# Attention values of two heads by turns, with the softmax sums divided out behind them

## The chip, the cores and the metric

The kernel runs on one core of a Trainium2 chip. The metric is the device time of one execution in microseconds, lower is better. The engines work side by side, each through its own list of instructions in a fixed order: TensorE (PE), VectorE (DVE), ScalarE (ACT), GpSimd (POOL), and SyncE (SP), which issues most DMAs.

## The reference

Sliding-window attention with a few sink keys, then two feed-forward layers, the first with a rational function, the second with a sigmoid. All in fp32.

```python
# q, k, v: 2 batches, 8 heads, 768 tokens, 64 wide; 4 sinks, window 128
scores = scale * np.matmul(q, k.transpose(0, 1, 3, 2))
keep = is_sink | in_window
scores = np.where(keep, scores, -1000000000.0)
scores = scores - np.max(scores, axis=-1, keepdims=True)
a = np.exp(scores)
a = a / (np.sum(a, axis=-1, keepdims=True) + 1e-09)
attn_out = np.matmul(a, v)
x = attn_out.transpose(0, 2, 1, 3).reshape(1536, 512)
# layer 1: w_in 512 x 2048, w_out 2048 x 512
h = x @ w_in
g = (a0 + a1*h + a2*h2 + a3*h3) / (1 + |b0|*|h| + |b1|*h2 + 1e-6)
x = g @ w_out
# layer 2, the same shapes
h = x @ w_in2
out = (h / (1 + np.exp(-1.702 * h))) @ w_out2
```

## The kernel before

The 1536 tokens are taken in three blocks of 512 (`TB`), each four query blocks of 128. Attention of a block runs over four pairs of heads. For a pair, `scores` multiplies the queries with the keys that a query block sees: its own 128, the 128 before and 16 sink columns, 272 in all (128 for the first query block of a batch). The two heads lie on the two halves of the 128 partitions and their scores are taken by turns. DVE adds the mask and takes the maximum (`m`, `nm`), ACT the exponential into `a` with its sum in `sm`. `normalise` adds a small number to the sums, takes the reciprocal `rs`, and multiplies every row of `a` by it, on DVE or POOL; the sink columns are also copied into a dense tile `as`. `transposes` turns blocks of 128 x 128 of `a` around on PE, three to a PSUM tile (`GROUP`), the sink tile as one more of them; ACT or DVE copy them into `th` and `sT`. `values` multiplies them with `vr`: output is 64 x 128 to 64 x 512, one head in the lower, one in the upper half of one PSUM tile, first all products of the one head, then all of the other, then the sinks of both. The result is split into a high part `xh` (ACT) and a rest `xl` (DVE) for the feed-forward layers (called MoE in the code), which multiply in three passes (high by high, high by rest, rest by high).

The layers run over units of one block and half or all of the 16 slices of the inner dimension (`UNITS`). Their weights arrive by DMA as 64-bit numbers (`wraw`), one tile of 512 KB at a time into two buffers, and are decoded on ACT (`dy`), DVE (`dy`, `dt`, and the rest into `wi` or `wo`) and one of three engines (the high part). The elementwise work of layer 1 (`y`, `z`, `s`, `r`, `gh`, `gl`) lies on ACT and DVE, with one DMA of POOL that adds.

The order of all instructions is found when the kernel is built: `play` goes through a list of operations with costs and priorities (the longest way to the end plus a number from `BIAS` for each group) and lets each engine start what is ready. That order is then written out for all five engines, SP's DMAs too. Some operations may go to one of several engines (`WH`, `SN`, `TH`, `S2`, `ST`); the plan decides. Where PE would have nothing in the first stage, the plan puts filler matmuls (`acc<-zero`, 256 columns) that only keep it busy. Extra buffers for the layers open once attention has ended. In tile names the number of the buffer is left out in the profile; in the order the number behind a name tells tiles apart.

Of the kernel before, what the change touches and what calls it, by code (L numbers as in the profile page):

```python
# [5 lines left out]
F32 = mybir.dt.float32  # L6
# [4 lines left out]
ALU = mybir.AluOpType  # L11
PSUM = bass.MemoryType.PSUM
DRAM = bass.MemoryType.DRAM
# [26 lines left out]
GROUP = 3  # L40
# [3 lines left out]
A_BUFS, M_BUFS, T_BUFS, VR_BUFS, KQ_BUFS = 4, 3, 6, 4, 2  # L44
# [5 lines left out]
TH, SN, PE_OUT = "act/dve", "pool/dve", "act/dve"  # L50

BIAS = {
# [4 lines left out]
}  # L57
HEAD = (5.08, 0.16, 15.06, 0.34)
THETA = -0.68
# [17 lines left out]
class View:  # L77
# [66 lines left out]
class Program:  # L144
# [56 lines left out]
    def op(self, eng, meth, alloc=(), alts=(), given=False, calls=(), cost=0.0, **kw):  # L201
# [18 lines left out]
        if calls:  # L220
            runs = [runner(eng, meth, c) for c in calls]
            o.alts = {eng: (cost, lambda: [f() for f in runs][-1])}
            o.cost, o.lat = cost, PE_LAT
            o.columns = sum(c["rhs"].n * 4 * (c["lhsT"].box[0][1] - c["lhsT"].box[0][0]) / P for c in calls)
        elif meth == "dma_start":
            v = views[0][1]
            o.nbytes = (v.box[0][1] - v.box[0][0]) * v.n * 4
            o.cost, o.lat = 0.45 if v.box[0][1] - v.box[0][0] == P else 0.62, DMA_LAT
            if eng == "gpsimd":
                o.nbytes *= 2  # L230
                o.cost, o.lat = ADD_FIX, ADD_LAT + 0.6 * (kw["out"].dtype == F32R)
            o.alts = {eng: (o.cost, runner(eng, meth, kw))}
        else:
            self.columns = 0
            o.alts = {e: (self.price(e, m_, k_), runner(e, m_, k_)) for e, m_, k_ in [(eng, meth, kw)] + list(alts)}
            o.cost = min(c for c, _ in o.alts.values())
            o.columns = self.columns
            if eng == "tensor":
                o.lat = PE_LAT
# [262 lines left out]
def emit(tc, qT, kX, vL, w_in, w_out, ca, cb, nw, out):  # L502
# [344 lines left out]
    def build_banded():  # L847
        with (
# [4 lines left out]
            tc.tile_pool(name="ps", bufs=1, space=PSUM) as ps,  # L853
        ):
# [16 lines left out]
            def attention(T, xs, alone):  # L871
# [28 lines left out]

                near = {k: [q for q in (k, (k[0], k[1] + 1)) if q in qcol] for k in kbs}
                n_g = -(-(sum(len(l) for l in near.values()) + bool(sq)) // GROUP)
                used = [0] * n_g
                place = {}
                for k in sorted(kbs, key=lambda k: -len(near[k])) + (["s"] if sq else []):
                    w = len(near[k]) if k != "s" else 1
# [39 lines left out]
                def scores(h):  # L946

                    kr, qr = st.pop(("kq", h // 2))
                    t = []
                    for e in (h, h + 1):  # L950
                        a = R.tile(ap, [P, 4, 2 * P + SC], F32, tag="a", name="a", bufs=A_BUFS)
                        nm = R.tile(ap, [P, 4], F32, tag="nm", name="nm", bufs=5)
                        sm = R.tile(ap, [P, 4], F32, tag="sm", name="sm", bufs=5)
                        st["a", e] = a, sm
                        t.append((slice((e % 2) * D, (e % 2 + 1) * D), a, nm, sm))
                    for i, (b, qb) in enumerate(qs):
                        off, w = (P + SC, P) if qb == 0 else (0, 2 * P + SC)
                        k0 = kcol[b, max(0, qb - 1)] * KW
                        ps_ = [pst("s") for _ in t]
                        R.op("tensor", "matmul", alloc=[x for y in t for x in y[1:]], cost=w / 420 + 0.11, calls=[  # L960
                            dict(out=p[:, :w], lhsT=qr[r, i * P:(i + 1) * P], rhs=kr[r, k0:k0 + w], start=True, stop=True)
                            for p, (r, _, _, _) in zip(ps_, t)])
                        for p, (_, a, nm, sm) in zip(ps_, t):
# [4 lines left out]
                            R.op("scalar", "activation", out=a[:, i, off:off + w], in_=mt[:, :w], func=AF.Exp, scale=-1.0,  # L968
                                 bias=nm[:, i:i + 1], accum_out=sm[:, i:i + 1])

                def normalise(h):
                    a, sm = st["a", h]
                    rs = R.tile(ap, [P, 4], F32, tag="rs", name="rs", bufs=2)
                    R.op("vector", "tensor_scalar", out=rs[:, :nq], in0=sm[:, :nq], scalar1=EPS_SM, scalar2=None, op0=ALU.add)
                    R.op("vector", "reciprocal", out=rs[:, :nq], in_=rs[:, :nq])
                    for i, (b, qb) in enumerate(qs):
                        off = P + SC if qb == 0 else 0
                        affine(SN, a[:, i, off:], a[:, i, off:], rs[:, i:i + 1], 0.0)
                    if sq:
                        i0, i1 = qcol[sq[0]], qcol[sq[-1]] + 1  # L980
                        s2 = R.tile(ap, [P, 4, 2 * SC], F32, tag="as", name="s2", bufs=2)
                        hi(S2, s2[:, :i1 - i0], a[:, i0:i1, P:P + 2 * SC])
                        st["s2", h] = s2[:, :i1 - i0]

                def transposes(h):
                    a, sm = st.pop(("a", h))
                    tr = []
                    for g in range(n_g):
                        t = R.tile(ap, [P, GROUP * P], F32, tag="th", name="th", bufs=T_BUFS)
                        p = pst("t")  # L990
                        w, ns = used[g] * P, 0
                        for k, (g2, at) in place.items():
                            if g2 != g:
                                continue
                            if k == "s":
                                ns = len(sq) * 2 * SC
                                R.op("tensor", "transpose", alloc=(t,), out=p[:ns, at * P:w], in_=st.pop(("s2", h)), identity=ident)
                                continue
# [3 lines left out]
                        if ns:  # L1002
                            w -= P
                            sT = R.tile(ap, [SC, 4 * P], F32, tag="sT", name="sT", bufs=2)
                            for j in range(len(sq)):
                                hi(ST, sT[:, j * P:(j + 1) * P], p[2 * SC * j:2 * SC * j + SC, w:w + P])
                            st["sT", h] = sT
# [4 lines left out]
                def values(h):  # L1012

                    x = pst("v")
                    calls, vrs = [], []
                    for e in (h, h + 1):
                        r0 = (e % 2) * D
                        p, tr, vr = x[r0:r0 + D], st.pop(("T", e)), st.pop(("v", e))
                        vrs.append(vr)
                        ops = []  # L1020
                        for k in first + later:
                            (g, at), n = place[k], len(near[k])
                            q0 = qcol[near[k][0]]
                            ops.append((p[:, q0 * P:(q0 + n) * P], vr[:, vcol[k], :], tr[g][:, at * P:(at + n) * P]))
                        for j, (o, l, r) in enumerate(ops):
                            calls.append(dict(out=o, lhsT=l, rhs=r, start=(j == 0), stop=(not sq and j == len(ops) - 1)))
                    if sq:
                        for e in (h, h + 1):
                            q0, n = qcol[sq[0]] * P, len(sq) * P
                            calls.append(dict(out=x[(e % 2) * D:(e % 2 + 1) * D, q0:q0 + n], lhsT=vrs[e % 2][:SC, vcol[sq[0][0], "s"], :], rhs=st.pop(("sT", e))[:, :n], start=False, stop=True))  # L1030
                    cost = sum(c["rhs"].n / 1100 + COL_EACH for c in calls)
# [166 lines left out]
```

## Time and profile before

| | us |
|---|---|
| median of 3 runs | 692.75 |
| lowest, highest | 690.96, 694.33 |
| profiled execution, its own time | 695.05 |
| its span, first to last instruction | 692.9 |
| mean granted clock of TensorE | 0.986 |

The page gives each engine's busy time. The table of windows gives the same by stretch, with the number of instructions; the timeline gives starts and durations in order of time (the distance from one start to the next is what an instruction costs its engine, since durations overlap); the groups give count, busy time and mean duration of instructions of one kind.

### The profile page before, as it was taken

To read this page: it belongs to the slowest core of one execution; us is meant where nothing else is said; L and a number is where in the kernel's file an instruction comes from. 1 tells how busy PE (TensorE), PEld (TensorE's weight loads), DVE (VectorE), ACT (ScalarE), POOL (GpSimd) and SP (SyncE) were. 2 spreads that over 40 slices of the span, in tenths; PEclk is the share of its full clock that TensorE was granted. 3 is DMA by queue.
4 is the path that set the end of the run, shared out by engine and by line. 5 is a ranking of instruction groups with operands and counts; after the bars stand their busy time and mean duration, and the time that the engine had idled before them with its cause. 6 is when DMAs were issued, how large, how long until landed. Compare 5 with 4: busy or idle time off the path is not lost.

```text
span 692.9 us, 9131 instructions
## 1 busy us (share of the span) xinstructions
PE 670.3 (97%) x3141; PEld 518.0 (75%) x3141; DVE 518.8 (75%) x1101; ACT 380.0 (55%) x786; POOL 102.2 (15%) x144
## 2 busy tenths in 40 slices
PE   7999999999999999999899999999999999999995
PEld 6776666677667787867687888788888888878874
DVE  5999999887686999997999999985488633131341
ACT  3686888687666775665767755543354422132220
POOL 1533342121121322111213100100000000000000
PEclk7999999999999999999999999999999999999998
DMA  5565766522211454344425324443033200010011
GB/s 164 172 188 148 197 171 165 128 68 53 54 32 30 92 125 104 77 107 122 86 66 140 58 60 118 124 125 92 17 105 122 62 1 0 1 48 13 16 46 64
DMA packets 29862, 61.69 MB, mean 89 GB/s; under 512 B 5744, under 2 KB 11888, under 8 KB 29808
## 3 DMA queue, kind: packets, MB, share of 16 engines
q1 hardware_dynamic: 22608, 48.44, 23.0%
q0 software_dynamic: 6912, 12.59, 10.8%
q8 instruction: 26, 0.43, 0.3%
q14 instruction: 28, 0.23, 0.1%
q10 hardware_dynamic: 288, 0.00, 0.0%
HBM read 45.29 MB, written 3.15 MB: 70 GB/s over the span
## 4 chain that ended last, share of the span: by engine, by line
PE 75%; DVE 7%; issue 6%; ACT 5%; DMA 5%; POOL 1%; SPq 0%; DVEq 0%; POOLq 0%; ACTq 0%
PE att L215 26%; PE acc L215 24%; PE h L215 19%; DMA z<-y 3%; PE att L216 3%; PE acc L863 2%; DVE s L216 2%; DVE dt L216 1%; ACT th L216 1%; DVE gl L216 1%; DMA q<-q_t 1%; ACT r L216 1%; DVE z L216 1%; ACT a L216 1%; ACT sT L216 1%
## 5 line engine op out<-in xcount | busy, mean ns | idle before, releaser
L215 PE MATMUL h<-xh,wi 128*128 128x512 f32 x448 | 151.5, 396 | 2.2 <-DVE s L216 1.7
L215 PE MATMUL att<-xh,wi 128*128 128x512 f32 x320 | 106.7, 391 | 0.0
L215 PE MATMUL acc<-gh,wo 128*128 128x512 f32 x288 | 100.6, 404 | 3.3 <-ACT wo L216 2.2
L215 PEld LDWEIGHTS h<-xh,wi 128*128 128x128 f32 x448 | 83.8, 188 | 26.1 <-issue 3.1
L216 DVE SCALAR_TENSOR_TENSOR dt<-wraw,dt 128x512 int32<-128x512 int32 x128 | 87.9, 688 | 1.4
L215 PE MATMUL h<-xl,wi 128*128 128x512 f32 x224 | 88.0, 393 | 0.0
L215 PE MATMUL acc<-wo,gh 128*128 128x512 f32 x256 | 83.2, 394 | 0.0
L216 DVE TENSOR_TENSOR gl<-y,gh 128x512 fp32r<-128x512 f32 x48 | 32.8, 689 | 66.7 <-PE acc L215 54.9
L215 PEld LDWEIGHTS att<-xh,wi 128*128 128x128 f32 x320 | 60.1, 188 | 14.2 <-DVE s L216 0.2
L216 POOL DMA_DIRECT2D z<-y x48 | 42.3, 887 | 192.5 <-ACT z L216 175.1
L215 PEld LDWEIGHTS acc<-gh,wo 128*128 128x128 f32 x288 | 53.6, 189 | 19.3 <-ACT wo L216 3.0
L215 PE MATMUL att<-xl,wi 128*128 128x512 f32 x160 | 62.5, 391 | 0.0
L216 ACT ACTIVATE dy<-wraw 128x512 f32<-128x512 f32 x64 | 42.9, 671 | 29.7 <-DMA wraw<-w_out 19.6
L216 ACT ACTIVATE a<-m,nm 128x272 f32<-128x272 f32 (+1 forms) x96 | 47.3, 496 | 19.1 <-DVE nm L216 18.9
L215 PE MATMUL acc<-gl,wo 128*128 128x512 f32 x144 | 55.5, 403 | 1.5 <-DVE gl L216 1.4
L215 PEld LDWEIGHTS acc<-wo,gh 128*128 128x128 f32 x256 | 48.0, 188 | 11.2 <-ACT wo L216 0.2
L216 ACT ACTIVATE r<-z,ln_b 128x512 f32<-128x512 f32 x48 | 34.6, 722 | 33.5 <-DMA z<-y 33.4
L216 ACT ACTIVATE gh<-y 128x512 fp32r<-128x512 f32 x48 | 30.2, 629 | 33.7 <-PE acc L215 25.2
L215 PEld LDWEIGHTS h<-xl,wi 128*128 128x128 f32 x224 | 42.1, 188 | 8.5 <-issue 0.4
L215 PE MATMUL att<-wo,gh 128*128 128x512 f32 x128 | 47.6, 396 | 0.4 <-POOL wo L216 0.3
L215 PE MATMUL acc<-wo,gl 128*128 128x512 f32 x128 | 45.6, 393 | 0.0
L216 DVE SCALAR_TENSOR_TENSOR gh<-s,a_t,r 128x512 fp32r<-128x512 f32 x48 | 36.0, 751 | 11.5 <-ACT r L216 10.5
(126 smaller groups left out, 1227.7 us busy)
## 6 DMA issues: line engine op xcount, KB each, us to landing
wraw<-w_in SPq DMA_DIRECT2D x32, 512.0 KB, 3.7
wraw<-w_out SPq DMA_DIRECT2D x32, 512.0 KB, 3.7
z<-y POOLq DMA_DIRECT2D x48, 256.0 KB, 3.3
vr<-v_l SPq DMA_DIRECT2D x16, 160.0 KB, 3.4
q<-q_t SPq DMA_DIRECT2D x8, 256.0 KB, 3.6
out<-xf SPq DMA_DIRECT2D x8, 256.0 KB, 2.4
k<-k_x SPq DMA_DIRECT2D x4, 360.0 KB, 3.1
k<-k_x SPq DMA_DIRECT2D x4, 288.0 KB, 5.0
```

The lines of the kernel that those rows point to most:

```text
L215: return getattr(e, meth)(a.pop("out"), **a)
L216: return getattr(e, meth)(**a)
L863: nc.tensor.matmul(R.real[k][:, 0:256], lhsT=zero[:, :P], rhs=zero, start=True, stop=True)
```

## The change

`values` takes the two heads by turns: product for product, first head, second head. The rows of `a` are no longer scaled; `normalise` is gone. Instead `sums` takes the reciprocals of the eight sums per partition of a pair (two heads, four query blocks), transposes them on PE to eight rows of 128, copies them to `rt`, writes them to DRAM (`rd`) and reads them back with two DMAs, each of which spreads one head's 512 numbers over 64 partitions (`rb`). DVE multiplies the values in PSUM by `rb`, and `xh` and `xl` are made from the product. `sinks` transposes the sink columns of each query block by themselves, straight from `a`, 32 columns at a time, into a PSUM tile of their own, so that one copy takes a pair (two copies where a block has four such query blocks). Four blocks go to one PSUM tile instead of three. There are fewer buffers for `m` and `th`; outside block 0 the transposes stand behind the pair's last scores. `BIAS`, `HEAD` and `THETA` have other numbers, so that the whole order differs.

```diff
-GROUP = 3
+GROUP = 4
-A_BUFS, M_BUFS, T_BUFS, VR_BUFS, KQ_BUFS = 4, 3, 6, 4, 2
+A_BUFS, M_BUFS, T_BUFS, VR_BUFS, KQ_BUFS = 4, 2, 4, 4, 2
-    "at0": 57.37, "at1": 40.94, "at2": -26.39, "at3": -86.3, "m0": -5.97, "m1": 87.68, "m2": 11.75,
+    "at0": 30.94, "at1": 72.58, "at2": 21.27, "at3": -64.03, "m0": -7.08, "m1": 59.83, "m2": 7.83,
...
+    def spread(self, n):
+        return View(self.t, self.box, self.dims, self.steps + [
+            lambda v: v.rearrange("(o a) b -> o (a b)", o=1).to_broadcast([n, v.shape[0] * v.shape[1]])], self.dtype)
...
-                def normalise(h):
-                    a, sm = st["a", h]
-                    rs = R.tile(ap, [P, 4], F32, tag="rs", name="rs", bufs=2)
-                    R.op("vector", "tensor_scalar", out=rs[:, :nq], in0=sm[:, :nq], scalar1=EPS_SM, scalar2=None, op0=ALU.add)
-                    R.op("vector", "reciprocal", out=rs[:, :nq], in_=rs[:, :nq])
-                    for i, (b, qb) in enumerate(qs):
-                        off = P + SC if qb == 0 else 0
-                        affine(SN, a[:, i, off:], a[:, i, off:], rs[:, i:i + 1], 0.0)
-                    if sq:
-                        i0, i1 = qcol[sq[0]], qcol[sq[-1]] + 1
-                        s2 = R.tile(ap, [P, 4, 2 * SC], F32, tag="as", name="s2", bufs=2)
-                        hi(S2, s2[:, :i1 - i0], a[:, i0:i1, P:P + 2 * SC])
-                        st["s2", h] = s2[:, :i1 - i0]
+                def sums(h):
+                    sm = st.pop(("sm", h))
+                    rs = R.tile(ap, [P, 8], F32, tag="rs", name="rs", bufs=2)
+                    R.op("vector", "tensor_scalar", out=rs, in0=sm, scalar1=EPS_SM, scalar2=None, op0=ALU.add)
+                    R.op("vector", "reciprocal", out=rs, in_=rs)
+                    p = pst("t")
+                    R.op("tensor", "transpose", out=p[:8, :P], in_=rs, identity=ident)
+                    rt = R.tile(ap, [8, P], F32, tag="rt", name="rt", bufs=2)
+                    hi(ST, rt, p[:8, :P])
+                    rd = R.tile(dp, [8, P], F32, tag="rd", name="rd", bufs=4)
+                    R.op("sync", "dma_start", out=rd, in_=rt)
+                    rb = R.tile(ap, [P, 4 * P], F32, tag="rb", name="rb", bufs=2)
+                    for e in (0, 1):
+                        R.op("sync", "dma_start", out=rb[e * D:(e + 1) * D], in_=rd[4 * e:4 * e + 4].spread(D))
+                    st["rb", h] = rb
+
+                def sinks(h):
+                    n, G = len(sq), 2 * SC
+                    t = R.tile(ap, [SC, 8 * P], F32, tag="sT", name="sT", bufs=1)
+                    for es in [(0, 1)] if n <= 2 else [(0,), (1,)]:
+                        p = pst("t")
+                        o = R.op("tensor", "transpose", alloc=(t,), cost=len(es) * n * 0.109 + 0.1, calls=[
+                            dict(out=p[:G, (i * n + j) * P:(i * n + j + 1) * P], in_=st["a", h + e][:, qcol[q], P:P + G], identity=ident)
+                            for i, e in enumerate(es) for j, q in enumerate(sq)])
+                        if not alone:
+                            R.in_order([st["last", h], o])
+                        hi(ST, t[:, es[0] * n * P:(es[-1] + 1) * n * P], p[:SC, :len(es) * n * P])
+                    st["sT", h] = t
...
                 def values(h):
...
+                    for k in first + later:
+                        (g, at), n = place[k], len(near[k])
+                        q0 = qcol[near[k][0]]
+                        ops += [(e, q0, n, vrs[e][:, vcol[k], :], tiles[e][g][:, at * P:(at + n) * P]) for e in (0, 1)]
...
                     n, c = nq * P, h // 2
-                    hi(XH, xs[0][c][:, :n], x[:, :n])
-                    lo("dve", xs[1][c][:, :n], x[:, :n], xs[0][c][:, :n])
+                    rb = st.pop(("rb", h))
+                    tt("dve", ALU.mult, rb, x[:, :n], rb)
+                    hi(XH, xs[0][c][:, :n], rb)
+                    lo("dve", xs[1][c][:, :n], rb, xs[0][c][:, :n])
...
-                        items.append(lambda h=2 * r - 2: (normalise(h), transposes(h), normalise(h + 1), transposes(h + 1), values(h)))
+                        items.append(lambda h=2 * r - 2: (sums(h), sinks(h) if sq else 0, transposes(h), transposes(h + 1), values(h)))
```

PE, the products of the first pair of block 0, before (`vr_62` and `vr_63` are the two heads):

```order
L215 MATMUL h_432<-th_379,vr_62 64x256
L215 MATMUL h_432<-th_388,vr_62 64x256
L215 MATMUL h_432<-th_396,vr_62 64x256
L215 MATMUL h_432<-th_379,vr_62 64x128
L215 MATMUL h_432<-th_406,vr_63 64x256
L215 MATMUL h_432<-th_418,vr_63 64x256
L215 MATMUL h_432<-th_416,vr_63 64x256
L215 MATMUL h_432<-th_406,vr_63 64x128
L215 MATMUL h_432<-sT_386,vr_62 64x256
L215 MATMUL h_432<-sT_411,vr_63 64x256
```

And now, the same products:

```order
L220 MATMUL h_348<-th_283,vr_62 64x256
L220 MATMUL h_348<-th_332,vr_63 64x256
L220 MATMUL h_348<-th_283,vr_62 64x256
L220 MATMUL h_348<-th_332,vr_63 64x256
L220 MATMUL h_348<-th_304,vr_62 64x256
L220 MATMUL h_348<-th_343,vr_63 64x256
L220 MATMUL h_348<-th_304,vr_62 64x128
L220 MATMUL h_348<-th_343,vr_63 64x128
L220 MATMUL h_348<-sT_309,vr_62 64x256
L220 MATMUL h_348<-sT_309,vr_63 64x256
```

The number and shape of the products are the same; their order goes from head after head to turn by turn. (One such row is two instructions in the trace.)

DVE in block 0 before, where the sums of one pair come in and rows of `a` are scaled between two weight decodes (`dt`):

```order
L216 TENSOR_SCALAR rs_289<-sm_283 128x4
L216 TENSOR_SCALAR dt_375<-dy_218 128x512
L216 RECIPROCAL rs_289<-rs_289 128x4
L216 TENSOR_SCALAR rs_285<-sm_294 128x4
L216 COPY sT_386<-att_357 16x128
L216 RECIPROCAL rs_285<-rs_285 128x4
L216 SCALAR_TENSOR_TENSOR dt_375<-wraw_64,dt_375 128x512
L216 TENSOR_SCALAR a_293<-a_293,rs_285 128x272
L216 SCALAR_TENSOR_TENSOR dt_375<-wraw_64,dt_375 128x512
L216 TENSOR_SCALAR a_282<-a_282,rs_289 128x272
```

And now, around the first multiplication by the spread reciprocals, which waits for its two DMAs:

```order
L221 SCALAR_TENSOR_TENSOR dt_233<-wraw_65,dt_233 128x512
L221 ISA m_207,nm_204<-acc_191,mk_125 128x272
L221 ISA nm_204 128x1
L221 TENSOR_TENSOR rb_390<-h_348,rb_390 128x512
L221 ISA m_203,nm_381<-acc_193,mk_125 128x272
L221 ISA nm_381 128x1
L221 SCALAR_TENSOR_TENSOR dt_233<-wraw_65,dt_233 128x512
```

The scalings are gone; the multiplication stands between score reductions (`m`) of later pairs and decode, so those stand behind it. Between the reciprocal of this pair and this row lie 9.5 us of other DVE work by the durations of the trace, 8.3 to 10.4 us for eleven of the twelve pairs and 5.0 us for the last.

SP in block 0 before, the loads of weights and of the next pair:

```order
L216 DMA k_181<-k_x 128x576
L216 DMA q_184<-q_t 128x512
L216 DMA wraw_64<-w_out 128x1024
L216 DMA vr_62<-v_l 128x320
L216 DMA vr_63<-v_l 128x320
L216 DMA wraw_65<-w_in 128x1024
```

And now, with the store and the two spreading loads of the first pair:

```order
L221 DMA wraw_65<-w_in 128x1024
L221 DMA rd_340<-rt_326 8x128
L221 DMA k_183<-k_x 128x576
L221 DMA q_186<-q_t 128x512
L221 DMA vr_62<-v_l 128x320
L221 DMA vr_63<-v_l 128x320
L221 DMA rb_390<-rd_340 64x512 x2
L221 DMA wraw_64<-w_out 128x1024
```

The store waits for ACT's copy, the loads for the store's landing, and the next weight load stands behind them. Of the 354 MoE matmuls that stood ahead of the last pair's values on PE, 159 still do; ahead of the eighth pair's, 75 instead of 73. Fillers go from 153 to 88.

## Rows read from the trace of the kernel before

**Rows 1.** The page: busy time of each engine, share of the span, instructions.

```profile
PE 670.3 (97%) x3141; PEld 518.0 (75%) x3141; DVE 518.8 (75%) x1101; ACT 380.0 (55%) x786; POOL 102.2 (15%) x144
```

**Rows 2.** Windows: from:to, length, busy us (instructions) by engine, clock, DMA, GB/s.

```profile
20.00:65.60 45.60, 45.19 (x304) 32.21 (x304) 44.56 (x143) 33.33 (x106) 20.73 (x30) 1.00 0.55 166
65.60:121.70 56.10, 54.44 (x321) 36.96 (x320) 54.14 (x164) 45.82 (x131) 18.97 (x27) 1.00 0.66 176
121.70:224.30 102.60, 101.04 (x504) 71.77 (x503) 79.18 (x195) 73.58 (x169) 17.05 (x25) 1.00 0.28 61
224.30:400.00 175.70, 168.77 (x717) 134.22 (x717) 167.83 (x275) 120.22 (x190) 38.37 (x45) 0.99 0.44 97
684.70:692.90 8.20, 0.00 (x0) 0.00 (x0) 1.81 (x4) 0.00 (x0) 0.00 (x0) 0.69 0.38 134
```

**Rows 3.** Timeline, DVE: the eighth pair's last operation (start, duration, instruction).

```profile
121.70 0.68 DVE L216 TENSOR_TENSOR xl<-att,xh 128x512 fp32r<-128x512 f32 x1
```

**Rows 4.** Timeline, PE: value products of one pair in blocks 0, 1 and 2.

```profile
41.70 2.65 PE L215 MATMUL h<-th,vr 128*64 128x256 f32 x16
44.28 0.65 PE L215 MATMUL h<-sT,vr 16*64 16x256 f32 x4
44.86 0.73 PE L215 MATMUL acc<-k,q 64*128 64x272 f32 x4
...
78.00 2.87 PE L215 MATMUL att<-th,vr 128*64 128x256 f32 x20
80.81 0.65 PE L215 MATMUL att<-sT,vr 16*64 16x256 f32 x4
81.38 0.73 PE L215 MATMUL att<-k,q 64*128 64x272 f32 x4
...
219.54 3.08 PE L215 MATMUL att<-th,vr 128*64 128x256 f32 x20
222.55 1.07 PE L215 MATMUL att<-sT,vr 16*64 16x512 f32 x4
223.56 0.50 PE L215 MATMUL h<-xh,wi 128*128 128x512 f32 x1
```

**Rows 5.** Timeline, PE: a sink transpose among the others, block 0.

```profile
49.34 0.27 PE L216 MATMUL att<-ident,a 128*128 128x128 f32 x1
49.45 0.27 PE L216 MATMUL att<-ident,as 128*64 128x128 f32 x1
49.56 0.49 PE L216 MATMUL att<-ident,a 128*128 128x128 f32 x3
```

**Rows 6.** Timeline, DVE: starts of operations one behind the other.

```profile
47.22 0.43 DVE L216 CUSTOM_DVE_ANT_0 m<-acc,mk 128x272 f32<-128x272 f32 x1
47.58 0.08 DVE L216 DVE_READ_ACCUMULATOR2_ANT nm<- 128x1 f32 x1
47.58 0.68 DVE L216 TENSOR_TENSOR xl<-h,xh 128x512 fp32r<-128x512 f32 x1
48.18 0.68 DVE L216 SCALAR_TENSOR_TENSOR dt<-wraw,dt 128x512 int32<-128x512 int32 x1
```

**Rows 7.** Groups of DVE up to 121.7 us: count, busy us, mean ns, idle before.

```profile
L216 DVE SCALAR_TENSOR_TENSOR dt<-wraw,dt 128x512 int32<-128x512 int32 x38 | 26.3, 695 | 0.2
...
L216 DVE TENSOR_SCALAR dy<-dy 128x512 f32<-128x512 f32 x19 | 8.5, 446 | 0.9 <-ACT dy L216 0.6
...
L216 DVE TENSOR_SCALAR a<-a,rs 128x272 f32<-128x272 f32 x17 | 7.8, 488 | 0.0
...
L216 DVE TENSOR_SCALAR a<-a,rs 128x128 f32<-128x128 f32 x9 | 3.0, 349 | 0.0
...
L216 DVE TENSOR_SCALAR rs<-sm 128x4 f32<-128x4 f32 x16 | 2.5, 180 | 0.0
```

**Rows 8.** The page, DMA issues: count, KB each, median us to landing.

```profile
out<-xf SPq DMA_DIRECT2D x8, 256.0 KB, 2.4
...
k<-k_x SPq DMA_DIRECT2D x4, 288.0 KB, 5.0
...
vr<-v_l SPq DMA_DIRECT2D x16, 32.0 KB, 2.1
...
b_t<-c_b ACTq DMA_DIRECT2D x1, 1.0 KB, 6.2
```

More of the change, by code (lines that the diff above doesn't have):

```diff
@@ L223, in op @@
             o.cost, o.lat = cost, PE_LAT
-            o.columns = sum(c["rhs"].n * 4 * (c["lhsT"].box[0][1] - c["lhsT"].box[0][0]) / P for c in calls)
+            o.columns = sum(c["rhs"].n * 4 * (c["lhsT"].box[0][1] - c["lhsT"].box[0][0]) / P if "rhs" in c else 2 * P for c in calls)
         elif meth == "dma_start":
@@ L853, in build_banded @@
             tc.tile_pool(name="ps", bufs=1, space=PSUM) as ps,
+            tc.tile_pool(name="dr", bufs=1, space=DRAM) as dp,
         ):
@@ L901, in attention @@
                 near = {k: [q for q in (k, (k[0], k[1] + 1)) if q in qcol] for k in kbs}
-                n_g = -(-(sum(len(l) for l in near.values()) + bool(sq)) // GROUP)
+                n_g = -(-sum(len(l) for l in near.values()) // GROUP)
                 used = [0] * n_g
                 place = {}
-                for k in sorted(kbs, key=lambda k: -len(near[k])) + (["s"] if sq else []):
-                    w = len(near[k]) if k != "s" else 1
+                for k in sorted(kbs, key=lambda k: -len(near[k])):
+                    w = len(near[k])
                     g = min((g for g in range(n_g) if used[g] + w <= GROUP), key=lambda g: used[g])
@@ L959, in scores @@
                         ps_ = [pst("s") for _ in t]
-                        R.op("tensor", "matmul", alloc=[x for y in t for x in y[1:]], cost=w / 420 + 0.11, calls=[
+                        o = R.op("tensor", "matmul", alloc=[sm] + [x for y in t for x in y[1:3]], cost=w / 420 + 0.11, calls=[
                             dict(out=p[:, :w], lhsT=qr[r, i * P:(i + 1) * P], rhs=kr[r, k0:k0 + w], start=True, stop=True)
                             for p, (r, _, _, _) in zip(ps_, t)])
-                        for p, (_, a, nm, sm) in zip(ps_, t):
+                        for p, (_, a, nm, s0) in zip(ps_, t):
                             mt = R.tile(ap, [P, 2 * P + SC], F32, tag="m", name="mt", bufs=M_BUFS)
@@ new lines, in scores @@
+                    st["last", h] = st["last", h + 1] = o
+                def sums(h):
+                    sm = st.pop(("sm", h))
+                    assert nq == 4
+                    rs = R.tile(ap, [P, 8], F32, tag="rs", name="rs", bufs=2)
[11 more added lines that the diff above has]
+                    st["rb", h] = rb
@@ L990, in transposes @@
                         p = pst("t")
-                        w, ns = used[g] * P, 0
+                        w = used[g] * P
+                        n0 = len(R.ops)
                         for k, (g2, at) in place.items():
                             if g2 != g:
[L994 to L997, printed above, removed]
                                 continue
@@ L1001, in transposes @@
                                 R.op("tensor", "transpose", alloc=(t,), out=p[:, (at + j) * P:(at + j + 1) * P], in_=a[:, qcol[q], o:o + P], identity=ident)
[L1002 to L1007, printed above, removed]
+                        if not alone:
+                            R.in_order([st["last", h], R.ops[n0]])
                         hi(TH, t[:, :w], p[:, :w])
@@ L1014, in values @@
                     x = pst("v")
[L1015 to L1026, printed above, removed]
@@ L1027, in values @@
-                    if sq:
[L1028 to L1031, printed above, removed]
+                    tiles = [st.pop(("T", e)) for e in (h, h + 1)]
+                    vrs = [st.pop(("v", e)) for e in (h, h + 1)]
@@ new lines, in values @@
+                    ops = []
+                    for k in first + later:
+                        (g, at), n = place[k], len(near[k])
+                        q0 = qcol[near[k][0]]
+                        ops += [(e, q0, n, vrs[e][:, vcol[k], :], tiles[e][g][:, at * P:(at + n) * P]) for e in (0, 1)]
+                    if sq:
+                        t, n = st.pop(("sT", h)), len(sq)
+                        for e in (0, 1):
+                            ops.append((e, qcol[sq[0]], n, vrs[e][:SC, vcol[sq[0][0], "s"], :], t[:, e * n * P:(e + 1) * n * P]))
@@ L1032, in values @@
+                    calls = [dict(out=x[e * D:(e + 1) * D, q0 * P:(q0 + n) * P], lhsT=l, rhs=r, start=(j < 2), stop=(j >= len(ops) - 2))
+                             for j, (e, q0, n, l, r) in enumerate(ops)]
+                    cost = sum(c["rhs"].n for c in calls) * 0.000845 + 0.12
                     R.op("tensor", "matmul", calls=calls, cost=cost)
                     n, c = nq * P, h // 2
-                    hi(XH, xs[0][c][:, :n], x[:, :n])
-                    lo("dve", xs[1][c][:, :n], x[:, :n], xs[0][c][:, :n])
+                    rb = st.pop(("rb", h))
```

16 lines of the change are left out of this document (8 added, 8 removed), and 6 rows, old and new, of the table BIAS.

## The prediction

> **What bounds the kernel now.** The busy shares come first: TensorE (PE) is busy 97% of the span [rows 1], which says little, since in the first 65 us it is fed with filler matmuls that only keep its clock up. So the second view is the table of busy time by stretch [rows 2], cut at events of the attention: 65.6 us ends block 0 (four pairs of heads), 121.7 us ends block 1 (the eighth pair; its last VectorE operation begins there [rows 3]), 224.3 us ends block 2. From 20 to 121.7 us VectorE (DVE) is busy 44.56 of 45.60 and 54.14 of 56.10 us: it is the bound, through softmax, weight decode and the scaling of the attention rows. From 121.7 to 224.3 us PE is busy 101.04 of 102.60 and DVE 79.18: PE is the bound. From 224.3 to 400 us both are near full (168.77 and 167.83 of 175.70); PE loses 6.9 us idle and 1% of its clock, 1.8 us. After that PE alone counts, to 684.7 us, and 8.20 us follow in which PE does nothing and the output leaves.
>
> So an edit pays in DVE time before 121.7 us, in PE time from there to 224.3 us, and in both, a little, up to 400 us.
>
> **The values by turns (PE).** Before, all products of the first head stand ahead of those of the second. A pair of block 0 starts its products at 41.70, its sink products at 44.28, and the scores after it at 44.86 us: 3.16 us [rows 4]. The sixteen instructions of the first part are twelve of 256 columns and four of 128; the four sink instructions of 256 columns, which already stand by turns, take 0.58 us, two at a time, so one 256-column instruction takes about 0.22 us with 0.15 us for the change into and out of this small form. One head alone has six of 256 and two of 128: 6 x 0.216 + 2 x 0.11 = 1.52 us. By turns both heads should take that, plus 0.06 to start, plus 0.58 of sinks: 2.16 us, 1.0 us less. Block 1 takes 3.38 us [rows 4] and becomes the same 2.15: 1.2 less. In block 2 a pair takes 4.02 us, 1.01 of it sinks [rows 4]; one head is 6 x 0.216 + 4 x 0.11 = 1.74, so 2.8 in all and 1.2 less. Does the second head really run beside the first? It does so already for a part: the first 16 instructions take 2.58 us where 12 x 0.216 + 4 x 0.11 = 3.03 would be needed one behind the other. I take full pairing.
>
> In blocks 0 and 1 PE has fillers and idle time, so these 8.8 us end nothing. In block 2, 4 x 1.22 = 4.9 us lie on the path.
>
> **The new transposes (PE).** Sinks go from two transposes a pair to eight in block 2 (four in the others), and one more carries the eight rows of reciprocals. A transpose follows the one before it after 0.11 us [rows 5]. Block 2 pays 4 x 6 x 0.11 = 2.6 us and 4 x 0.2 = 0.8 us. Their outputs are 32 and 8 rows high. The narrow sink transpose of before (64 rows) followed a full one and started 0.11 us after it, with no gap [rows 5]; so I put nothing for the change of form, and at most the 0.15 us above for each of 12 groups, 1.8 us, as the other end. The Trainium skill, in "TensorEngine Tiling (Array Packing)", Key Properties, says that a change of tiling mode drains TensorE; by that the sum would be 1.8 us longer. The trace shows no drain at the 64-row transposes, and no run here shows 8 or 32 rows. Block 2: -4.9 + 2.6 + 0.8 = **-1.5 us**.
>
> **The scaling (DVE, up to the eighth pair).** An operation takes about 0.08 us less of DVE than its own duration, since the next starts early: a 0.43 us reduction is followed after 0.36, a 0.68 us subtraction after 0.60 us [rows 6]. The order says how many of each stand ahead of the eighth pair's last operation, durations are in [rows 7]:
> scalings of 272 columns, 17 x (0.488 - 0.08) = -7.0; of 128 columns, 9 x 0.27 = -2.4; sums and reciprocals, 32 to 17 of about 0.1 = -1.4. The multiplication of the values by the spread reciprocals adds 8 x 0.60 = +4.8.
> The order also moves work: score reductions of 272 columns 28 to 35, 7 x 0.36 = +2.5; three more 512-column elementwise operations, +1.8; and fewer weights are decoded by then: 8 of 38 combining operations (0.61), 4 and 4 of the two light ones (0.37) and 2 subtractions (0.60), -9.1. These are not saved; they move to block 2, where DVE has had 23 us idle. Small copies cancel to under 1 us. Sum: **-10.8 us**. PE stands equally far at this point (75 matmuls of the MoE against 73), so the end of block 1 moves by this. Removed scalings of GpSimd (47) end nothing: that engine is far from full. I take 1 us back for new waits: **-10 us**.
>
> **After attention.** With block 2 ahead of only 159 instead of 354 MoE matmuls, some 195 of them, about 46 us of PE at 0.236, and nine steps of elementwise DVE work, about 34 us, move behind it. The share of DVE there falls from 167.83 of 175.70 (0.96) to (168 + 34) / (176 + 46) = 0.91. So the 8.7 us that PE loses there should shrink; bounds are none and all, I take half: **-4 us**.
>
> **Sum.** 692.9 - 10 - 1.5 - 4 = 677.4 us of span. The profiled execution took 695.05, 2.15 more than its span; the median is 692.75, 2.3 less. So 677.4 + 2.15 - 2.3 = **677 us**.
>
> **What the new chain must fit into.** The reciprocals now go PE, ScalarE (ACT), out to DRAM, back to 64 partitions twice, then DVE. Between a reciprocal and its multiplication the order puts, for eleven of twelve pairs, 8.3 to 10.4 us of DVE work (5.0 for the last). The chain: about 0.7 us for reciprocal, transpose and copy, 0.45 for the second issue, and two landings. The nearest rows are 2.1 us for 32 KB and 5.0 for a load in traffic [rows 8]: 5.4 to 11.2 us; I take 2.5 to 3.5 a landing, as these are small, and nothing waits. The stores to DRAM of before landed in 2.4 us. The Trainium skill, "DMA: Bandwidth & Descriptors", Anatomy of one DMA, puts a fixed cost of about 2 us on any DMA and calls the receipt of a write to HBM its heaviest part; it speaks against going through DRAM. Here the trace has its own rows, and the first rival is what the rule would do.
>
> **Rivals.**
> *The round trip is late (slower).* DVE works in its written order: behind a late multiplication stand score reductions and decode, and behind the two loads on SyncE's queue the next weight load. If a landing takes 5.6 us, between the 5.0 and the 6.2 of the broadcast b_t [rows 8], the chain is 12.4 us against about 9.4: 3 us for each of eight pairs, 24 us, 701 us. It decides from about 5.1 us a landing: there the chain is 11.4 us, and 2 us x 8 eat the gain. Against it: small loads land in 2.1. Chance 0.16, half of it near no change.
> *ACT takes over in blocks 0 and 1.* It was busy 33.33 and 45.82 us there [rows 2], its exponentials remain, and the score buffers go from three to two. By the order its own work falls by some 3 us only (wider copies, but as many exponentials), so 10 becomes 3: 684 us. Chance 0.09.
> *The heads do not run together.* Then block 2 pays +3.4 instead of -1.5 and little is gained later: 692.9 - 10 + 3.4 - 1, or 685 us. Chance 0.04.
> *All gaps go.* The 8.7 us vanish and no wait comes: 692.9 - 10.8 - 1.5 - 8.7, or 672; with the last idle of DVE ahead of 121.7 us (3.0) gone too, 669. Chance 0.11.
>
> **How the numbers follow.** The forecast (672 to 684) has 0.60. The range runs from 667 to 689: it takes in the last three rivals and leaves out the late round trip. About 0.5% is what a measurement can tell from no change, 689.3 to 696.2: faster 0.84, same 0.08, slower 0.08.
>
> **What would show it.** Right: the eighth pair's last DVE operation about 10 us earlier; value groups of about 2.15, 2.15 and 2.8 us; block 2 over near 160 us; DVE above 95% until the eighth pair; landings of the new loads below 4 us. Wrong: DVE idle until the DMA of rb; SyncE held with a weight load behind it; ACT fuller than DVE before 110 us; value groups still above 3 us; a PE idle time between 160 and 400 us as large as before.

## The result

| | before | after |
|---|---|---|
| median of 4 runs, us | 692.31 | 676.61 |
| lowest, highest | 690.96, 694.33 | 675.01, 677.00 |
| profiled execution, its own time | 695.05 | 675.01 |
| its span | 692.9 | 673.0 |
| mean granted clock of TensorE | 0.986 | 0.993 |

The ratio is 0.9766 (0.9737 to 0.9796): 16 us less. The two profiled executions lie 20 us apart, because the one of after lies 1.6 us below its median and the one of before 2.7 above; milestones below come from these two traces.

The page of after, busy time by engine, against [rows 1]:

```profile
PE 652.1 (97%) x3128; PEld 499.3 (74%) x3128; DVE 502.3 (75%) x1019; ACT 373.3 (55%) x734; POOL 66.8 (10%) x86
```

Windows of after, cut at the same events as [rows 2] (from:to, length, busy us by engine, clock, DMA share, GB/s):

```profile
20.00:55.40 35.40, 33.97 (x250) 22.33 (x248) 32.10 (x103) 28.99 (x86) 2.98 (x4) 1.00 0.70 209
55.40:112.10 56.70, 55.44 (x355) 36.43 (x354) 53.75 (x155) 46.94 (x128) 6.96 (x9) 1.00 0.71 191
112.10:161.20 49.10, 48.10 (x307) 31.08 (x307) 39.89 (x104) 35.72 (x91) 3.42 (x4) 1.00 0.44 123
161.20:400.00 238.80, 233.50 (x1007) 187.58 (x1006) 224.13 (x369) 167.98 (x263) 45.40 (x51) 1.00 0.41 90
400.00:665.20 265.20, 264.78 (x1135) 209.66 (x1133) 138.68 (x237) 84.08 (x142) 5.31 (x6) 1.00 0.17 54
```

Block 0 ends 10.2 us earlier; DVE is busy there 32.10 of 35.40 us, 91%, below the 95% that the prediction named as a sign. Block 1 takes as long as before (56.70 against 56.10 us) with PE and DVE again nearly full. Block 2 takes 49.1 instead of 102.6 us, because so much less of the layers stands ahead of it. The eighth pair's last DVE operation, [rows 3] of before, begins 9.6 us earlier:

```profile
112.09 0.69 DVE L221 TENSOR_TENSOR xl<-rb,xh 128x512 fp32r<-128x512 f32 x1
```

The value groups of after on PE, one of each block, against [rows 4]; the distance between starts is the cost:

```profile
42.83 1.73 PE L220 MATMUL h<-th,vr 128*64 128x256 f32 x16
44.49 0.65 PE L220 MATMUL h<-sT,vr 16*64 16x256 f32 x4
45.07 0.50 PE L220 MATMUL att<-k,q 64*128 64x272 f32 x2
```
```profile
62.23 1.74 PE L220 MATMUL att<-th,vr 128*64 128x256 f32 x20
63.89 0.65 PE L220 MATMUL att<-sT,vr 16*64 16x256 f32 x4
64.47 0.50 PE L220 MATMUL att<-k,q 64*128 64x272 f32 x2
```
```profile
117.98 1.95 PE L220 MATMUL att<-th,vr 128*64 128x256 f32 x20
119.86 1.07 PE L220 MATMUL att<-sT,vr 16*64 16x512 f32 x4
120.87 0.50 PE L220 MATMUL att<-k,q 64*128 64x272 f32 x2
```

They take 2.24, 2.24 and 2.89 us instead of 3.16, 3.38 and 4.02. The transpose of the eight reciprocal rows among full ones, against [rows 5]:

```profile
60.28 0.27 PE L221 MATMUL att<-ident,rs 128*8 128x128 f32 x1
60.39 0.49 PE L221 MATMUL att<-ident,a 128*128 128x128 f32 x3
```

The next starts after 0.11 us, and the sink transposes, 32 rows high, follow each other at that distance too. In "TensorEngine Tiling (Array Packing)", Key Properties, the Trainium skill says that a change of tiling mode drains TensorE; at this change of output height the trace shows no such time, and the 1.8 us that I had as the other end are not there.

The new round trip, the tile `rb` of after: what DVE waited for in front of the multiplications (us, times), and the landings (us, shortest, median, longest), against [rows 8]:

```profile
  DMA rb<-rd: 2.9, 4
...
DMA to landing us min/median/max: 3.2/4.6/5.3
```

### The profile page after: what moved, and what is told of

Read it like the earlier page. It is cut to its first block, busy times and chain, and to the rows that moved or that the text cites. A ratio compares the mean times of both kernels' runs of the same rounds, so it can differ in the third digit from the quotient of the medians.

```text
span 673.0 us, 8941 instructions
## 1 busy us (share of the span) xinstructions
PE 652.1 (97%) x3128; PEld 499.3 (74%) x3128; DVE 502.3 (75%) x1019; ACT 373.3 (55%) x734; POOL 66.8 (10%) x86
## 4 chain that ended last, share of the span: by engine, by line
PE 73%; DVE 11%; DMA 6%; issue 5%; ACT 3%; POOL 1%; SPq 0%; DVEq 0%; POOLq 0%; ACTq 0%
PE att L220 26%; PE acc L220 24%; PE h L220 18%; DMA z<-y 4%; PE att L221 4%; DVE s L221 3%; DVE dt L221 3%; PE acc L869 1%; DVE z L221 1%; DMA q<-q_t 1%; ACT r L221 1%; DVE gh L221 1%; DVE gl L221 1%; DMA wraw<-w_out 1%; DVE wo L221 1%
## 5 line engine op out<-in xcount | busy, mean ns | idle before, releaser
L220 PE MATMUL h<-xh,wi 128*128 128x512 f32 x416 | 142.7, 397 | 0.5 <-POOL wi L221 0.3
L220 PE MATMUL att<-xh,wi 128*128 128x512 f32 x352 | 116.6, 392 | 0.3 <-DVE y L221 0.3
L220 PE MATMUL acc<-gh,wo 128*128 128x512 f32 x272 | 93.5, 399 | 1.6 <-DVE gh L221 1.6
L220 PEld LDWEIGHTS h<-xh,wi 128*128 128x128 f32 x416 | 77.9, 188 | 19.6 <-issue 1.8
L220 PE MATMUL acc<-wo,gh 128*128 128x512 f32 x288 | 91.4, 396 | 0.2
L220 PE MATMUL h<-xl,wi 128*128 128x512 f32 x208 | 82.1, 395 | 0.0
L220 PEld LDWEIGHTS att<-xh,wi 128*128 128x128 f32 x352 | 66.1, 188 | 16.1 <-DVE y L221 1.1
L220 PE MATMUL att<-xl,wi 128*128 128x512 f32 x176 | 68.8, 391 | 0.0
L220 PEld LDWEIGHTS acc<-wo,gh 128*128 128x128 f32 x288 | 53.3, 188 | 14.0 <-ACT gh L221 2.1
L220 PE MATMUL att<-gh,wo 128*128 128x512 f32 x112 | 40.2, 394 | 1.8 <-ACT xh L221 1.8
```

What stands on the lines that cost most here:

```text
L220: return getattr(e, meth)(a.pop("out"), **a)
```

## Experiments

Pair by pair, I compare when the last DVE operation (`xl`) of the fourth, eighth and twelfth pair begins: 65.6, 121.7 and 224.3 us before, 55.4, 112.1 and 161.2 after. Each comes from one trace; a second trace of the changed kernel (`a0_changed`, below) has them within 0.1 us. "Order kept" means that `BIAS`, `HEAD` and `THETA` stay and that an edit alters instructions after the plan has set their places.

### The two edits in the old order

**Values by turns alone** (e1_turns), in the kernel before, order kept:

```diff
+m = len(first + later)
+calls = [calls[e * m + j] for j in range(m) for e in (0, 1)] + calls[2 * m:]
```

> The kernel before with one edit: the value products of the two heads stand by turns; every other instruction keeps its place in the order. Theory (what bounds differs by stretch): value groups shrink from 3.16, 3.38 and 4.02 us to about 2.24, 2.25 and 2.89 us, some 12.7 us of TensorE in all, but blocks 0 and 1 are bound by VectorE, so only the 4 x 1.13 us of block 2 shorten the run: 4 to 6 us less than before, ratio about 0.993. Rival 1 (TensorE bounds everywhere): about 13 us less, ratio 0.982. Rival 2 (the heads do not run together by the turn alone, the other edits do it): groups unchanged, ratio 1.000.

Measured: 690.72 against 693.17 us, ratio 0.9971 (0.9942 to 0.9999), 2 us less. A group of block 0, for one, shrinks as it should:

```profile
41.38 1.73 PE L215 MATMUL h<-th,vr 128*64 128x256 f32 x16
43.04 0.65 PE L215 MATMUL h<-sT,vr 16*64 16x256 f32 x4
43.62 0.73 PE L215 MATMUL acc<-k,q 64*128 64x272 f32 x4
```

But the milestones are 65.4, 122.3 and 222.1: nothing is gained by the eighth pair, 2 us in block 2. In block 1 PE now stands idle for 6.7 us instead of 1.7, while DVE is as full as before:

```profile
65.40:122.30 56.90, 50.20 (x319) 33.77 (x320) 54.25 (x165) 45.66 (x131) 19.08 (x27) 1.00 0.63 173
```

The instruction gain is real, and less of it reaches the end than I had put.

**No scaling at all** (e2_no_scaling), in the kernel before, order kept; the 96 multiplications by `rs` are left out:

```diff
+o = R.ops[-1]
+o.alts = {e: (c, lambda: None) for e, (c, _) in o.alts.items()}
```

> The kernel before without the 96 multiplications of attention rows by the reciprocal sums (49 on VectorE, 47 on GpSimd); every other instruction keeps its place, the values come out unscaled. Theory (VectorE bounds blocks 0 and 1): 17 and 9 of them stood on VectorE ahead of the eighth pair's last operation, 9.4 us of it, so that point comes about 9 us earlier and the run is 8 to 11 us shorter, ratio about 0.986. Rival (the scalings are covered, and ScalarE or the chain of a pair bounds): under 3 us, ratio above 0.996.

Measured: 689.98 us, 0.9952 (0.9929 to 0.9975), 3.3 us less. Milestones 61.4, 117.1 and 219.6: 4.2 us are won in block 0, and in block 1 almost nothing more. Its windows, blocks 0 and 1:

```profile
20.00:61.40 41.40, 41.40 (x284) 29.78 (x284) 37.90 (x123) 32.08 (x100) 5.03 (x9) 1.00 0.56 172
61.40:117.10 55.70, 54.44 (x323) 37.30 (x322) 49.11 (x151) 45.63 (x131) 7.65 (x9) 1.00 0.63 178
```

DVE falls from 54.14 to 49.11 us in block 1, and the block stays 55.7 us long: PE is as full as before, 54.44 us. How much of that could give way is shown by the windows of the kernel before for the fillers' tile `zero` alone (PE, PEld, DVE):

```profile
20.00:65.60 45.60, 16.17 (x100) 12.99 (x100) 0.00 (x0) 1.00 0.55 166
65.60:121.70 56.10, 4.25 (x26) 3.22 (x24) 0.00 (x0) 1.00 0.66 176
```

Fillers are 16 us of block 0 but only 4.25 of block 1, and in a written order they keep their places. So in block 1 two engines were nearly full, and each stands in the way when the other alone is relieved.

**GpSimd's share of the scalings left out alone** (e3_no_pool_scaling; 47 of the 96), in the kernel before, order kept:

> The kernel before without the 47 scalings on GpSimd alone; those on VectorE stay, every other instruction keeps its place, and a part of the values comes out unscaled. Theory (GpSimd is far from full, its scalings end nothing): ratio 0.998 to 1.000. Rival (the scaling's latency, 0.53 us each four times a head ahead of the transposes, is on the path): 3 us or more less, ratio 0.996 or below.

Measured: 690.90 us, 0.9967 (0.9944 to 0.9989); milestones 63.7, 118.8 and 222.2. So I was wrong that they end nothing: taking work off an engine that is 15% busy moves the fourth pair by 1.9 us and the eighth by 2.9, more than half of what all 96 are worth there. The trace shows a reason of that size: the scalings that stay on DVE become shorter. Up to 121.7 us, against 7.8 us and 488 ns each in [rows 7]:

```profile
L216 DVE TENSOR_SCALAR a<-a,rs 128x272 f32<-128x272 f32 x17 | 5.4, 349 | 0.0
```

That is 2.4 us, and the scalings of 128 columns and the copies `as` give 0.8 more. PE's waits for rows scaled by GpSimd came to only 0.4 us in blocks 0 and 1 of the kernel before. By what the two engines hinder each other is not shown.

**Both edits** (e10_both), in the kernel before, order kept, asks whether PE and DVE held each other up:

> The kernel before with the values by turns and without the 96 scalings, both in the old order (values unscaled). Alone the one gave 2.0 and the other 3.3 us. Theory (in block 1 VectorE and TensorE bound each other, so either alone leaves the other in the way): more than the sum of the two, 7 to 11 us less than before, ratio 0.984 to 0.990. Rival (the fixed order keeps what is saved): the sum, 5 us or less, ratio 0.993 or more.

Measured: 687.85 against 692.60 us, 0.9956 (0.9925 to 0.9988): 3 us by the ratio, 5 by the medians, no more than the two edits' own gains added up. Milestones 63.0, 118.1 and 218.6. Block 1, the whole window and then a piece of the chain in it:

```profile
63.00:118.10 55.10, 49.75 (x319) 33.83 (x320) 49.48 (x151) 45.43 (x131) 7.07 (x9) 1.00 0.63 179
```
```profile
70.51 0.27 PE att L216
70.80 0.49 ACT th L216
71.30 0.65 ACT a L216 x3
...
78.33 0.57 ACT dy L216
78.96 0.31 issue
79.27 0.75 DVE dt L216 x2
```

PE and DVE have each lost 4.7 us in the block, and it is 1.0 us shorter. No engine is full: in this piece the chain steps from PE to ACT, stays there for eight microseconds of copies, exponentials and decode in their written places, goes to DVE, and back. In the old order most of the work that the edits save does not turn into time.

### The same edits, the old numbers; the old kernel, the new numbers

**The changed kernel with before's `BIAS`, `HEAD` and `THETA`** (e4_old_numbers), planned anew:

> The changed kernel with the numbers of the kernel before in BIAS, HEAD and THETA: all edits of the computation stay, the order is planned anew from the old numbers. Theory (the gain is in the removed VectorE and TensorE time, the numbers fit the order to it): most of the gain stays, 678 to 685 us, ratio 0.979 to 0.990. Rival 1 (the numbers alone carry the gain): ratio 1.000 or above. Rival 2 (the numbers carry nothing): ratio 0.975 to 0.979.

Measured: 691.62 us, 0.9976 (0.9955 to 0.9998): 1.7 us less, far from what I expected. **The kernel before with the new numbers** (e9_new_numbers):

> The kernel before with the numbers of the changed one in BIAS, HEAD and THETA and nothing else: block 2's attention ends behind 168 MoE matmuls instead of 354. Theory (work removed and order need each other: with the scaling still on VectorE and head after head on TensorE the early attention costs what the later stretch gives back): 685 to 695 us, ratio 0.990 to 1.004. Rival 1 (the numbers alone carry the gain): 676 to 682 us. Rival 2 (they fit only the changed kernel): over 698 us.

Measured: 704.38 us, 1.0156 (1.0122 to 1.0189): 11.8 us *slower*. The edits alone win 2 us, the numbers alone lose 12, both together win 16. Where it goes is seen in the stretch from 250 to 400 us, one window each of before, after, e4_old_numbers and e9_new_numbers:

```profile
250.00:400.00 150.00, 143.24 (x607) 113.64 (x606) 142.51 (x233) 101.62 (x161) 30.43 (x35) 0.99 0.43 94
```
```profile
250.00:400.00 150.00, 145.72 (x628) 116.83 (x627) 144.63 (x244) 103.04 (x161) 24.53 (x29) 1.00 0.42 92
```
```profile
250.00:400.00 150.00, 139.96 (x586) 111.17 (x586) 143.48 (x240) 99.24 (x157) 28.52 (x33) 0.98 0.43 97
```
```profile
250.00:400.00 150.00, 139.35 (x571) 109.98 (x570) 140.46 (x237) 99.15 (x156) 28.03 (x32) 0.95 0.44 104
```

In equal time PE starts 607, 628, 586 and 571 matmuls. e4 is as quick as after up to the eighth pair (54.9 and 111.5 us), with 289 instead of 159 matmuls of the layers ahead of block 2's end, and then loses it: its 800th such matmul starts at 331.7 us, after's at 311.9, before's at 334.2. e9 is through block 2 early (179.0) with blocks 0 and 1 hardly quicker than before (64.4, 120.3), and pays in the layers. A wait of PE in e9 (start, duration, instruction, idle time before it), and the clock behind it:

```profile
380.68 0.79 PE L215 MATMUL h<-xh,wi 128*128 128x512 f32 x1 [3.02 <-DVE s L216]
```
```profile
381.00:384.50 3.50, 3.50 (x9) 2.73 (x9) 3.50 (x7) 2.82 (x5) 0.90 (x1) 0.50 0.44 75
```

After 3.0 us of idle time the granted clock is 0.50, the lower level, 1.2 GHz; so a late DVE costs PE its wait and a slow stretch behind it.

**Which numbers?** (e11_old_at) Only `at0` to `at3`, the priorities of attention, set back in the changed kernel:

```diff
-    "at0": 30.94, "at1": 72.58, "at2": 21.27, "at3": -64.03,
+    "at0": 57.37, "at1": 40.94, "at2": -26.39, "at3": -86.3,
```

> The changed kernel with the four attention numbers at0 to at3 of the kernel before: block 2's attention ends behind 264 MoE matmuls instead of 159. Theory (ending attention early is what frees VectorE in the later stretch): most of the gain goes, 685 to 692 us, ratio 0.990 to 1.000. Rival (it is the MoE's numbers): 676 to 680 us.

Measured: 694.09 us, 1.0006 (0.9987 to 1.0024): the whole gain is gone. By the trace, which is of the slowest of its ten executions (698.82 us), 264 layer matmuls stand ahead of block 2's end, which comes at 198.0 us, and PE waits again, for instance

```profile
349.50 0.50 PE L220 MATMUL att<-gl,wo 128*128 128x512 f32 x1 [2.54 <-DVE gl L221]
```

The counterpart (e12_old_moe), `at0` to `at3` as changed and before's other numbers of `BIAS` (units, weights) back:

> The changed kernel with its own attention numbers and all other numbers of BIAS as in the kernel before (HEAD and THETA stay new): block 2's attention ends behind 149 MoE matmuls. Theory (ending attention early is what counts): most of the gain stays, 676 to 683 us, ratio 0.976 to 0.987. Rival (it is the MoE's numbers): 685 to 692 us.

Measured: 681.26 us, 0.9835 (0.9795 to 0.9875): 11 of the 16 us stay. Block 2 ends at 159.0 us behind 149 layer matmuls. What it lacks against after is mostly one wait and the slow stretch behind it, with a granted clock of 0.56:

```profile
294.07 0.50 PE L220 MATMUL h<-xh,wi 128*128 128x512 f32 x1 [4.24 <-DVE s L221]
```
```profile
294.00:297.50 3.50, 3.15 (x7) 2.08 (x8) 3.50 (x7) 1.20 (x2) 0.00 (x0) 0.56 0.47 157
```

So the four attention numbers carry most of the gain, given the edits. Block 2 ends at 161.2 and 159.0 us where the gain is there, at 202.0 (e4) and 198.0 us (e11) where it is not. That this early end carries it, and not something else that the four numbers move (e11's eighth pair comes at 115.0 instead of 112.1), is my reading. How single numbers act on each other stays open.

### The parts inside the changed kernel

These ran beside the changed kernel once more (a0_changed):

> The changed kernel once more, as the measure for the three beside it: 676 to 677 us, ratio 0.974 to 0.980.

It took 675.96 us, 0.9753 (0.9731 to 0.9775).

**Heads one after the other again** (e5_heads), order kept:

```diff
+ops.sort(key=lambda o: o[0])
```

> The changed kernel with the value products of the first head ahead of those of the second again; every other instruction keeps its place in the new order. Value groups should go from 2.24, 2.25 and 2.89 us back to about 3.2, 3.4 and 4.0 us, 12.7 us of TensorE. Theory (in the new order TensorE bounds block 2 and is near its limit in block 1): 5 to 9 us more than the changed kernel, ratio to before 0.984 to 0.990. Rival 1 (as in the old order, where the turns alone gave 2 us): 2 us more. Rival 2 (TensorE bounds all of attention now): 12 us more, ratio 0.995.

Measured: 683.19 us, 0.9866 (0.9846 to 0.9886), 7.2 us slower than the changed kernel. Milestones 56.8, 115.5 and 168.3 against 55.3, 112.0 and 161.3: 1.5 us are lost in block 0, 2.0 in block 1 and 3.5 in block 2. Here the pairing pays in all blocks; in the old order it paid 2 us.

**The loads of `rb` made independent of the store** (e6_rb_free; they read 64 rows of an input array instead of one stored row 64 times, so the values are multiplied by other numbers), order kept:

```diff
+out=v.real(), in_=kX[0, 0, e * D:(e + 1) * D, 0:4 * P]
```

> The changed kernel with the spread tile rb read from an input array instead of the stored sums: the same two loads of the same size at the same places, but no wait for the store's landing, and no wait of SyncE for it; the values come out multiplied by other numbers. Theory (the round trip fits but for the 3.8 us that VectorE sat idle ahead of five multiplications): 1 to 4 us less than the changed kernel. Rival (loads that leave earlier and SyncE set free bring the weights earlier too): over 5 us less.

Measured: 675.48 us, 0.9758 (0.9734 to 0.9782): 0.5 us less, which is no difference. DVE still waits, and the loads land no sooner:

```profile
  DMA rb<-k_x: 2.6, 4
...
DMA to landing us min/median/max: 2.8/4.5/6.2
```

The store's landing was hardly waited for even in the changed kernel, because other entries of SP's list stand between store and loads. SP's waits for it there (us in total, times, longest), and the first pair's store and loads:

```profile
SPq L221 <- DMA rd<-rt: 3.6, 5, 0.9
```
```profile
21.58 0.35 SPq L221 DMA_DIRECT2D rd<-rt  x1
...
24.83 0.80 SPq L221 DMA_DIRECT2D vr<-v_l  x2
25.73 1.14 SPq L221 DMA_DIRECT2D rb<-rd  x2
```

What is left of DVE's wait is the loads' late place on SP and their own landing. Spreading one row is not what makes that landing long, since these loads of 64 rows take as long.

**One more copy of 4 KB from DRAM to DRAM** (e7_two_hops) between store and loads, order kept:

```diff
+if e == 0:
+    nc.sync.dma_start(out=rd2, in_=rd.real())
```

> The changed kernel with one more copy in DRAM between the stored sums and the spread tile, twelve DMAs of 4 KB on SyncE's queue: the chain grows by one landing, 2 to 3 us. Theory (the slack behind the multiplications is used up in blocks 0 and 1, as VectorE already waits there): up to 3 us for each of eight pairs, 10 to 22 us more than the changed kernel, about 687 to 699. Rival (VectorE catches up elsewhere, since TensorE bounds): under 5 us more.

Measured: 695.77 us, 1.0072 (1.0040 to 1.0104), 19.8 us slower than the changed kernel and slower than before. The tile `rb`, DVE's idle time, and SP's waits (us in total, times, longest):

```profile
  DMA rb<-rd: 14.4, 7
  DVE rb L221: 11.0, 5
```
```profile
SPq L1000 <- DMA rd<-rd: 26.5, 12, 4.2
```

DVE waits 14.4 instead of 2.9 us, ACT 11.0 instead of 4.6 us for DVE's product behind that. On SP's queue the loads wait 26.5 us for twelve copies, 2.2 each behind 0.5 to issue, with the weight loads behind them. Milestones 62.4, 127.7 and 180.3: some 2.7 us more in a chain of about eleven takes the whole gain. How much of it comes by DVE's wait and how much by the weights behind it on SP was not separated.

## Why the prediction was right, and where its steps were not

The time (677 said, 676.6 measured) and the direction came out, and both edits do what was said of their instructions. That the time fits within 0.4 us is luck in part: the first stage was counted too low and the gaps behind attention too high, and the two errors cancel.

**The scaling, -10 us to the eighth pair: the sum was met, but its terms are not separate gains.** The operation began 9.6 us earlier. But the list mixed work that goes away (scalings -9.4, smaller reductions -1.4, the new product +4.8) with work that the order moves (decode -9.1, score reductions and elementwise +4.3). Without the scalings alone, the old order moved by 4.6 us, about half, and 2.9 of these came with GpSimd's 47, of which I had said that they end nothing: 2.4 of the 7.0 us that I booked for DVE's long scalings were the price of GpSimd working beside them. "In blocks 0 and 1 PE has fillers and idle time, so these 8.8 us end nothing" held in the old order (e1) and failed in the new one, where e5 finds the pairing worth 3.5 us by the eighth pair, 2.0 of them in block 1. Fillers are 4.25 and idle is 1.66 of 56.10 us there before, so PE had at most 6 us to give. The table in [rows 2] already showed it at 54.44 beside DVE's 54.14; I named the one and took the other for padding.

**"PE stands equally far" was wrong in size.** I counted 75 against 73 matmuls up to the last values in PE's order. By the time of DVE's operation, PE had started 92 of the layers' matmuls after, 79 before: 13 x 0.232 = 3.0 us. It had also done more of block 2's attention: what was left fell by 5.0 us (32.8 to 27.8), and 3.5 of these are sixteen score products and four transposes done earlier. With 9.6 that makes 16.1 us of the 19.5 by which PE's end moves between the traces (684.7 to 665.2).

**Block 2 on PE, -1.5:** by the distances of PE's starts the products take 4.5 us less instead of 4.9, the transposes 3.0 more instead of 3.4 (the four of the reciprocals 0.2 instead of 0.8), so the sum stays at -1.5. Both heads do run together, and the third rival falls; e5, which puts them apart, gives 683.19 us, near its 685, but half of its 7.2 us arise before block 2, where the rival put nothing.

**After attention, -4: at most -2.** Of the 19.5 us, 1.9 are left for this term (19.5 - 16.1 - 1.5). Between block 2's end and 400 us PE's idle time falls from 6.93 to 5.30 us, and the 1.8 us of lower clock are absent from this trace. Behind 400 us some of it is lost again: before, 1233 matmuls started in 284.70 us, after, 1135 in 265.20, 0.231 and 0.234 us each, about 3 us in all, for a reason not looked into. My reason, a smaller share of DVE, also held only loosely: 224.13 of 238.80 is 0.94, not 0.91. That these gaps depend on the order of the layers and not on DVE's share alone is what e12 shows, with one wait of 4.24 us and the clock behind it.

So 16.1 and 1.5 + 1.9 us in the traces stand against 10 and 1.5 + 4. The traces differ by 4.2 us more than the medians do (19.9 against 15.7). The second trace of the changed kernel, with the same milestones, is 1.4 us longer: PE stands idle for 1.9 us between 350 and 360 us there, and the granted clock is 0.83 over the next 10 us. The kernel before was traced once, with such a slow stretch in it. So this excess lies at least in part behind block 2, in the term after attention, which by the medians may be near nothing.

**The round trip: the chain mis-sized, the rival near.** I took 2.5 to 3.5 us for a landing; the median of the loads is 4.6, in the row of the page

```profile
rb<-rd SPq DMA_DIRECT2D x24, 128.0 KB, 4.6
```

where the point of decision was 5.1. The nearer row of [rows 8] was the 5.0 of a load in traffic, not the 2.1 of the small load. The chain as a whole was longer still than I had summed, 6.1 to 8.1 us. In the four pairs whose multiplication waited, it began 10.4 to 11.8 us behind its reciprocal; in the first, the store left 1.8 us behind the reciprocal, the first load 4.2 us behind the store, and the multiplication began 5.0 us later. What I had left out is the loads' place on SP behind entries that wait for other things. DVE had 9.4 to 10.7 us of other work meanwhile, and so the wait stayed at 2.9 us in all. "Nothing waits" failed by that much, and e6 shows that the store's landing has no measurable part in it. e7 shows that the rival's mechanism is about as steep as worked out: 24 us were named for 3 us more, and 19.8 were measured for some 2.7. The Trainium skill, "DMA: Bandwidth & Descriptors", Anatomy of one DMA, gives a fixed cost of about 2 us, fitted on the path of GpSimd's DMAs, which the prediction took for any DMA. On SP's queue the trace is near it for e7's 4 KB copy, at 2.2 us of SP's wait, and not for the loads of `rb`, at 4.6.

**Not foreseen: that the change needs its order.** I took the new numbers as a way to make room, and forecast e4 at 678 to 685. Edits and new numbers earn little or lose each by itself, 1.7 and -11.8 us, and earn 16 together. My reading of the runs: the edits make attention cheap enough that block 2 can go ahead of the layers without starving them. e9 and e11 show both halves of it; that no other order would serve the old computation as well was not tried.

## What to carry to other kernels

Where a plan writes the order of all engines, what an operation costs and what its removal saves are two figures: look which engine stands next to the bound, subtract fillers from its busy share, ask whether an operation is long only because of a neighbour engine, and do not book as saved what only moves. An edit and the order that it allows are to be measured crosswise, since each by itself may win nothing or lose. A round trip through DRAM is bearable where some ten microseconds of other work stand between its ends, with its landings sized by loads of like size in like traffic, the entries ahead of them on the issuing queue counted, and the price of one landing more found out.

## What the runs showed of the hardware

- A load that spreads 2 KB over 64 partitions (128 KB written) lands in 4.6 us (median) under traffic, and one that reads 64 rows of 2 KB and waits for no store in 4.5; I had put 2.5 to 3.5.
- Without GpSimd's scalings beside them, DVE's scalings of 272 columns took 349 instead of 488 ns each, and the run ended 2.3 us earlier though GpSimd was 15% busy.
- After idle times of 3.0 and 4.2 us on PE, the granted clock was 0.50 and 0.56 over the 3.5 us behind them.
- Products of two heads (128 rows, 64 columns, fp32) issued by turns took 2.24 us a pair in block 0, head after head 3.16.
